# Requesting each weight piece of a fused attention and gated-MLP kernel as two transfers of unequal partition ranges

## The chip, the cores and the metric

The kernel runs on one core of one Trainium2 chip. The metric is the device time of one execution in microseconds (us). Three runs of the kernel before gave 142.08, 142.20 and 143.18 us; their median is 142.2 us.

## The reference, cut to what matters

```python
def _attn_ref(q, k, v, alpha):            # 4 batches, 8 heads, 768 steps, 48 wide
    state = zeros((B, H, D, D)); y = zeros_like(q)
    for t in range(S):
        state = alpha[:, :, t, :, None] * state + einsum('bhd,bhe->bhde', k[:, :, t], v[:, :, t])
        y[:, :, t] = einsum('bhd,bhde->bhe', q[:, :, t], state)
    return y

def _moe_ref(x, w_in, w_spatial, b_spatial, w_out):   # x is y as (4, 768, 384)
    h = maximum(x @ w_in, 0.0)                        # w_in (384, 1024)
    u, v = h[..., :512], h[..., 512:]
    v_n = (v - mean(v)) / sqrt(var(v) + 1e-06)        # over the last axis
    v_s = einsum('ts,bsd->btd', w_spatial, v_n) + b_spatial[None, :, None]   # w_spatial (768, 768)
    return (u * v_s) @ w_out                          # w_out (512, 384)
```

All inputs and the output are float32.

## The kernel before, in words

The first half is a gated linear attention. It is computed in 24 chunks of 128 steps, six to each of the four batches. For each chunk the kernel reads alpha (tile `ac`), k (`kc`), q (`qc`) and v (`vc`). The first eight chunks are read two at a time, with 384 KB in a request (L432); the others are read singly, with 192 KB (L637). ScalarE takes the logarithm of alpha (`la`), TensorE sums it over time, ScalarE makes exponentials of the sums (`binvp` or `binv`), GpSimd or VectorE scales k with them (`kt`), VectorE scales q (`qt`), TensorE transposes both, multiplies them (`ptm` is the masked product), and carries a running state from chunk to chunk (`state`, `sbd`).

The second half is a gated MLP on the four batches: x times `w_in` (columns 512 to 1023 give v, columns 0 to 511 give u), a normalisation of v, a product with `w_spatial` over time, a bias, a product with u, and a product with `w_out`. It is interleaved with the attention of later chunks.

The weights are read once, in six pieces of 768 KB each: the half of `w_in` for v, then the half for u, then `w_spatial` in three pieces of 256 rows, then `w_out` (L1067 to L1073). The function `fetch` (L1076) handles one piece. Its inner function `load` (L1081) takes a tile named `raw_w` of 128 partitions and 6 KB a partition, and requests the whole piece with one DMA on the SP queue (L1084). The source is a view of 128 partitions by n rows: n is 3 with runs of 512 numbers (2 KB) for `w_in`, 2 with runs of 768 numbers (3 KB) for `w_spatial`, and 4 with runs of 384 numbers (1.5 KB) for `w_out`. Then n copies (`cast`, L1090) turn the piece into bf16, one for each of the n rows, on ScalarE, VectorE or GpSimd. Each cast covers all 128 partitions. The pool `raws` has two buffers for `raw_w` (L160, NRAW = 2), so the third piece can be requested only when the casts of the first are done, and so on. After the last piece the same buffers serve as output tiles. The `w_spatial` casts give rows named `w_row`, which TensorE transposes at L831 into `w_spT`; the spatial product of the first batch needs them all.

The order of the instructions on every engine is written out by hand. The string PLAN (L57) is a list of words such as `S109 Q110`: a letter for the engine and the number of an operation. `replay` (L112) issues the operations in that order. An operation that requests a DMA is an S word, and the SP queue issues its requests in the order of the S words. The six weight pieces stand at places 10, 15, 18, 19, 24 and 31 of the 111 requests of the SP queue. All other requests of that queue are reads of ac, kc, qc and vc and stores of the output. The requests use eight completion semaphores in turn: each request waits, on the SP queue, until the request eight places before it has landed. An instruction that reads a tile waits for the semaphore of the request that filled it.

Of the kernel before, what the change touches and what calls it, by code (L numbers as in the profile page):

```python
# [124 lines left out]
def kernel(  # L125
# [12 lines left out]
    nc = tc.nc  # L138
# [57 lines left out]
    def copy(eng, out, in_):  # L196
        if eng == "ACT":
            nc.scalar.copy(out=out, in_=in_)  # L198
        else:
            ENG[eng].tensor_copy(out=out, in_=in_)  # L200
# [84 lines left out]
    def op(key, *args, **kw):  # L285

        users = kw.pop("use", ())
        o = Op(key, *args, **kw)
        for s in users:
            s.users.append(o)  # L290
        ops.append(o)
        made[key] = o
        return o

    def got(*keys):
        return [made.get(x) for x in keys]

    def dma(key, us, emit, deps, prio, eng="SP", issue=0.99, lat=1.9):
        o = op(key + ("issue",), eng, issue, emit, deps, prio=prio)
        return op(key, "DMA", us, lambda _: None, [o], prio=prio, lat=lat)  # L300
# [775 lines left out]
    def fetch(key, prio, to, src):  # L1076

        n, cols = src.shape[1], src.shape[2]
        hold = {}

        def load(_):  # L1081
            flat = raws.tile([128, n * cols], FP32, name="raw_w")
            hold["w"] = flat.rearrange("p (n f) -> p n f", n=n)
            nc.sync.dma_start(out=hold["w"], in_=src)  # L1084

        dma(key, WT, load, list(fetched[-NRAW] if len(fetched) >= NRAW else []), prio, issue=0.68)
        for j in range(n):
            tt = 2 * key[-1] + j if to is None else None

            def cast(eng, j=j, tt=tt):  # L1090
                if to is None:
                    wsp_nat[tt] = raws.tile([128, S], BF16, name="w_row", bufs=NROW)
                copy(eng, wsp_nat[tt] if to is None else to[:, j, :], hold["w"][:, j, :])

            op(("cast",) + key + (j,), {"POOL": 0.02 + 0.0012 * cols, "ACT": 0.11 + 0.00073 * cols, "DVE": 0.07 + 0.00104 * cols},
               None, cast, got(key), prio=prio + 12)
            if to is None:
                casts.append((made[("cast",) + key + (j,)], tt))
        made[key] = [made[("cast",) + key + (j,)] for j in range(n)]
        fetched.append(made[key])  # L1100
# [59 lines left out]
```

## Time and profile before

| What | Value |
|---|---|
| median of three runs | 142.2 us (142.08 to 143.18) |
| the profiled execution, its own time | 142.43 us |
| span of the profiled execution, first to last instruction | 140.6 us |
| time around the span | 1.8 us |
| granted TensorE clock, mean | 0.997 of full speed |
| TensorE (PE) busy | 135.3 us, 96% of the span |
| VectorE (DVE) busy | 118.5 us, 84% |
| ScalarE (ACT) busy | 108.1 us, 77% |
| GpSimd (POOL) busy | 83.9 us, 60% |
| moved by DMA | 28.64 MB, mean 204 GB/s |

All times in the profile are microseconds from the start of the span unless marked ns. The busy figure of TensorE includes matmuls on a tile named `junk`, whose results nobody reads. PE is TensorE's matmul, PEld its weight load, and SPq is the queue that issues the requests. A row of the timeline gives start, duration, engine, source line, operation, tiles (written, then read), shape, count, and in brackets the idle time of the engine before it and what ended that idle time. For a request on SPq the duration is the time that it held the queue; the time from its start to its landing stands in the view of DMA issues. The row of 40 digits gives, for 40 equal slices of the span of 3.5 us each, how busy something was in tenths.

### The profile page before, as it was taken

Reading aid. Unit: us, or ns where it says so; the run is one execution under the profiler, and the core shown is the slowest. Engines: PE = TensorE matmul, PEld = TensorE weight load, DVE = VectorE, ACT = ScalarE, POOL = GpSimd, SP = SyncE. Lnnn points to the kernel's source line nnn. Section 1 sums busy time; section 2 is a strip of 40 time slices with the busy share of each in tenths; the row PEclk is TensorE's granted clock in tenths of the full one; section 3 lists DMA queues with packets and bytes.
Section 4 is the critical chain, followed back from the end, with each engine's and each line's share of the span. In section 5 each row is a group of like instructions: output and inputs, shape, how many; then the busy total and the mean of one; then the engine's idle time right before and its main releaser. Section 6 shows DMA issues by size and latency. Waiting matters only on the chain.

```text
span 140.6 us, 4974 instructions
## 1 busy us (share of the span) xinstructions
PE 135.3 (96%) x1921; PEld 84.1 (60%) x1921; DVE 118.5 (84%) x292; ACT 108.1 (77%) x279; POOL 83.9 (60%) x148
## 2 busy tenths in 40 slices
PE   7999999999999999999999999999999999999990
PEld 3357566574767656665665765656657666566560
DVE  7187799989999789899689999999899899987850
ACT  3487898899976678999989699989967978751021
POOL 6816458861469996970289999402788599002520
PEclk9999999999999999999999999999999999999998
DMA  4999997989999979989999998999999120005535
GB/s 101 320 324 328 338 254 245 295 286 315 267 226 161 306 145 215 203 175 210 188 199 190 188 200 171 199 200 220 257 222 225 71 107 7 0 23 212 215 146 192
DMA packets 89000, 28.64 MB, mean 204 GB/s; under 512 B 83728, under 2 KB 87440, under 8 KB 88976
## 3 DMA queue, kind: packets, MB, share of 16 engines
q1 hardware_dynamic: 88944, 28.32, 81.8%
q8 instruction: 15, 0.25, 0.7%
q14 instruction: 9, 0.07, 0.2%
q0 software_dynamic: 32, 0.00, 0.0%
HBM read 23.60 MB, written 4.72 MB: 201 GB/s over the span
## 4 chain that ended last, share of the span: by engine, by line
PE 59%; ACT 9%; DMA 9%; SPq 7%; POOL 5%; DVE 5%; issue 4%; ACTq 0%; POOLq 0%
PE bank L819 42%; SPq L432 7%; DMA raw_w<-in_moe_w_in_dram 5%; DMA ac<-in_alpha_dram 3%; PE bank L710 3%; PE bank L745 2%; PE bank L773 2%; PE bank L731 2%; PE bank L657 2%; PE bank L767 1%; POOL kt L681 1%; DMA out_dram<-raw_w 1%; PE bank L389 1%; POOL kt L474 1%; ACT vn L880 1%
## 5 line engine op out<-in xcount | busy, mean ns | idle before, releaser
L819 PE MATMUL bank<-w_spT,vn 128*128 128x384 bf16 x192 | 35.9, 326 | 0.0
L980 POOL TENSOR_TENSOR gT<-vsb,uT 128x384 bf16<-128x384 f32 x27 | 25.0, 939 | 12.5 <-DVE vsb L967 12.1
L819 PEld LDWEIGHTS <-vn 128*128 128x128 bf16 x192 | 17.3, 97 | 10.2
L681 POOL TENSOR_TENSOR kt<-kc,binv 128x384 bf16<-128x384 f32 x16 | 14.6, 917 | 11.9 <-ACT bc L676 7.3
L756 DVE TENSOR_TENSOR ptm<-bank,mask 128x512 bf16<-128x512 f32 x32 | 20.5, 680 | 0.7 <-PE bank L745 0.6
L819 PE MATMUL bank<-xT,w_in 128*128 128x384 bf16 x96 | 19.9, 326 | 0.0
L967 DVE TENSOR_TENSOR vsb<-bank,bsp_bc 128x384 f32<-128x384 f32 x31 | 16.6, 551 | 3.6 <-PE bank L819 3.0
L819 PE MATMUL bank<-w_in,xT 128*128 128x512 bf16 x72 | 18.8, 379 | 0.3 <-ACT xT L198 0.2
L819 PE MATMUL bank<-w_out_sb,gT 128*128 128x384 bf16 (+1 forms) x100 | 18.6, 320 | 0.0
L198 ACT COPY kqT<-bank 128x512 bf16<-128x512 bf16 x28 | 15.9, 598 | 2.2 <-PE bank L710 1.5
L335 POOL TENSOR_TENSOR state<-state,bc 128x192 f32<-128x192 f32 x20 | 10.1, 506 | 12.4 <-DVE mvs L896 5.5
L200 POOL CAST sbd<-state 64x192 bf16<-64x192 f32 x40 | 13.7, 341 | 2.1
L204 ACT ACTIVATE v_sb<-bank 128x512 bf16<-128x512 f32 x20 | 12.0, 602 | 2.4 <-PE bank L819 2.3
L884 DVE BATCH_NORM_STATS2 stats<-v_sb 128x6 f32<-128x512 bf16 x20 | 13.6, 682 | 0.0
L204 ACT ACTIVATE uT<-bank 128x384 bf16<-128x384 f32 x23 | 10.9, 492 | 2.2 <-PE bank L819 2.0
L819 PEld LDWEIGHTS <-w_in 128*128 128x128 bf16 x96 | 8.7, 97 | 5.9
L198 ACT COPY xT<-bank 128x192 bf16<-128x192 bf16 (+1 forms) x25 | 9.0, 377 | 4.1 <-PE bank L389 2.9
L819 PEld LDWEIGHTS <-gT 128*128 128x128 bf16 x100 | 8.8, 97 | 5.0
L188 PE MATMUL bank<-junk 128*128 128x512 f32 (+6 forms) x22 | 10.7, 613 | 1.1 <-DVE junk L1050 1.1
L585 DVE TENSOR_TENSOR ptm<-bank,mask 128x512 bf16<-128x512 f32 x16 | 10.3, 682 | 1.0 <-PE bank L574 1.0
L198 ACT CAST x_sb<-bank 128x384 bf16<-128x384 f32 x19 | 9.0, 494 | 2.3 <-PE bank L773 2.3
L916 DVE TENSOR_SCALAR vn<-v_sb,mvs,rstd 128x512 bf16<-128x512 bf16 x24 | 8.9, 404 | 1.5 <-ACT rstd L909 1.5
(129 smaller groups left out, 281.2 us busy)
## 6 DMA issues: line engine op xcount, KB each, us to landing
ac<-in_alpha_dram SPq DMA_DIRECT2D x16, 192.0 KB, 4.0
kc<-in_k_dram SPq DMA_DIRECT2D x16, 192.0 KB, 4.0
qc<-in_q_dram SPq DMA_DIRECT2D x16, 192.0 KB, 4.2
vc<-in_v_dram SPq DMA_DIRECT2D x16, 192.0 KB, 4.0
raw_w<-in_moe_w_spatial_dram SPq DMA_DIRECT2D x3, 768.0 KB, 5.5
out_dram<-raw_w SPq DMA_DIRECT2D x11, 192.0 KB, 2.9
out_dram<-o_sb SPq DMA_DIRECT2D x9, 192.0 KB, 1.9
ac<-in_alpha_dram SPq DMA_DIRECT2D x4, 384.0 KB, 4.6
```

What stands on the lines that cost most here:

```text
L188: nc.tensor.matmul(out=flat[:, 0:cols].rearrange("p (a b) -> p a b", a=4), lhsT=junk, rhs=junk[:, None, 0:n].to_broadcast([128, 4, n]), st ...
L198: nc.scalar.copy(out=out, in_=in_)
L200: ENG[eng].tensor_copy(out=out, in_=in_)
L204: nc.scalar.activation(out=out, in_=in_, func=AF.Relu)
L335: ENG[eng].tensor_tensor(out=st["state"], in0=st["state"], in1=st["bc"][:, :, None].to_broadcast([128, HP, D]), op=ALU.mult)
L585: nc.vector.tensor_tensor(out=st[f"ptm{par}"][:, s], in0=st[f"pt{s}{par}"], in1=mask2[:, par], op=ALU.mult)
L681: ENG[eng].tensor_mul(out=k_blocks(kt3)[:, :, :, 0:D], in0=quad(st["kc"]), in1=st["binv"])
L756: nc.vector.tensor_tensor(out=st["ptm"][:, s], in0=st[f"pt{s}"], in1=mask4, op=ALU.mult)
L819: return lambda ps: nc.tensor.matmul(out=out(ps), lhsT=lhsT(), rhs=rhs(), start=start, stop=stop)
L884: nc.vector.bn_stats(out=stats, in_=d["v_sb"][:, tt, :])
L967: nc.vector.tensor_tensor(out=hold["vs"], in0=ps[:, 0:TH], in1=bsp_bc[:, th, :], op=ALU.add)
L980: ENG[eng].tensor_tensor(out=bt[b]["gT"][:, dsl, cols], in0=hold["vs"], in1=bt[b]["uT"][:, dsl, cols], op=ALU.mult)
```

## The change

In `load`, the one request of a piece becomes two, of partitions 0 to 79 and of partitions 80 to 127. Both write the same `raw_w` tile. Everything else stays: the string PLAN, the buffers, the casts and their engines.

```diff
         def load(_):
             flat = raws.tile([128, n * cols], FP32, name="raw_w")
             hold["w"] = flat.rearrange("p (n f) -> p n f", n=n)
-            nc.sync.dma_start(out=hold["w"], in_=src)
+            for rows in (slice(0, 80), slice(80, 128)):
+                nc.sync.dma_start(out=hold["w"][rows], in_=src[rows])

         dma(key, WT, load, list(fetched[-NRAW] if len(fetched) >= NRAW else []), prio, issue=0.68)
```

A piece of 768 KB is then requested as 480 KB and 288 KB, back to back. The SP queue has 117 requests in place of 111. No other engine's instructions change in number, shape or order; each cast waits for two completion semaphores in place of one, and because six requests more take part in the turn of eight semaphores, every later request waits for a request that lies fewer places back in the old count where weight requests lie in between.

## The prediction

> **What bounds the kernel now.** I read the page first, for the slices of the span and the chain that ended last.
>
> ```profile
> DMA  4999997989999979989999998999999120005535
> PE bank L819 42%; SPq L432 7%; DMA raw_w<-in_moe_w_in_dram 5%; DMA ac<-in_alpha_dram 3%; PE bank L710 3%; PE bank L745 2%; PE bank L773 2%; PE bank L731 2%; PE bank L657 2%; PE bank L767 1%; POOL kt L681 1%; DMA out_dram<-raw_w 1%; PE bank L389 1%; POOL kt L474 1%; ACT vn L880 1%
> ```
>
> The reader is to see that the DMA engines are full up to slice 31 (109 us) and that one weight transfer, the first half of w_in, stands on the chain. The chain in order of time says where.
>
> ```profile
> 10.29 6.88 DMA raw_w<-in_moe_w_in_dram
> 17.19 0.62 ACT w_in L198
> ...
> 34.12 0.95 DVE w_row L200 x2
> 35.12 0.52 PE bank L831 x24
> 35.64 1.08 PE bank L819 x6
> ```
>
> So the start is paced by transfers, up to the first weight cast at 17.19. From there a run of ScalarE, GpSimd and VectorE work leads to the transposes of w_spatial at 35.12, and then TensorE is the chain almost without a break to 62 us. What delays the casts before 43 us delays TensorE. Next the timeline, for the casts that wait for a piece, and the SP queue's rows.
>
> ```profile
> 17.19 0.62 ACT L198 CAST w_in<-raw_w 128x512 bf16<-128x512 f32 x1 [0.34 <-DMA raw_w<-in_moe_w_in_dram]
> ...
> 26.22 0.61 POOL L200 CAST w_in<-raw_w 128x512 bf16<-128x512 f32 x1 [0.25 <-DMA raw_w<-in_moe_w_in_dram]
> ```
>
> ```profile
> 10.29 1.33 SPq L1084 DMA_DIRECT2D raw_w<-in_moe_w_in_dram  x1
> 11.66 0.49 SPq L432 DMA_DIRECT2D kc<-in_k_dram  x1
> 12.20 1.06 SPq L432 DMA_DIRECT2D qc<-in_q_dram  x1
> 13.31 3.73 SPq L432 DMA_DIRECT2D vc<-in_v_dram  x1
> ```
>
> The two idle times, 0.34 and 0.25 us, are all that an earlier landing of w_in could give back. The queue issues far ahead of the data: the qc requested at 12.20 lands 8.0 us later.
>
> **Where a piece lands.** The view of DMA issues, window by window, gives the time from issue to landing. I add it to the issue's start. The alpha before the first piece lands at 9.02 + 5.0 = 14.0, the piece at 10.29 + 6.9 = 17.2: 3.2 us for 768 KB. The second (alpha 17.16 + 5.4 = 22.6, piece 18.28 + 7.8 = 26.1) takes 3.5. The first w_spatial piece (kc 20.64 + 7.8 = 28.4, piece 23.25 + 7.2 = 30.4) takes 2.0. The second (28.78 + 4.3 = 33.1) comes 2.7 later, about 0.65 of it because its request waited for a cast. So a piece needs 2.0 us of the DMA engines at best, and the w_in pieces 1.2 and 1.5 more.
>
> **The change part by part.**
>
> *Six more issues on SP.* The shortest rows of a weight issue and of its neighbour are 0.37 and 0.43 us, so 6 x 0.4 = 2.4 us of the SP queue. I cost them at nothing: behind the first piece the requests land 6.6 to 8.0 us after issue, behind the second w_spatial piece 5.1, so the DMA engines have several transfers in hand while SP issues. If that cover were gone it would be 0.4 each, 2.4 in all.
>
> *The turn of eight semaphores.* With the extra requests, a request waits for one that lies six or seven places back in the old count. The closest case I find is the qc at 35.54, which would wait for the second w_spatial piece's second half; the whole piece landed at 33.1, so 2.4 us are spare. Cost nothing; should the landing come over 2.4 us later than SP, it is that excess.
>
> *A second wait on each cast.* The parts land in order, so the first has landed when the second does. Nothing, apart from the instruction that carries the wait.
>
> *The transfers themselves.* No row of this trace shows a transfer of 80 or of 48 partitions. From below: five stores of 192 KB, issued back to back from 128.48 to 130.46, land between 128.48 + 4.0 = 132.5 and 130.46 + 3.9 = 134.4, so 768 KB in four requests take 1.9 us. By that row a further request is free: 0. A gain is limited by the idle times above to 0.34 + 0.25 = 0.6 us in all. From above: each part takes as long as a whole good piece, so 2.0 us more. Between them I take 0.8 us more for each piece: nearer to the lower end because the first w_spatial piece shows no loss beside the best rate, and not at it because the w_in reads, in the same queue, show that a request can lose 1.2 to 1.5 us over that rate; two requests of unequal size have two such occasions.
>
> *How 0.8 us reaches the end.* I keep two sums: how late the queue is, and how late the engines are.
> 1. First w_in piece: the cast starts when it lands. Queue 0.8, engines 0.8.
> 2. Second w_in piece: queue 1.6. GpSimd's cast starts 0.1 after landing, and GpSimd has 0.2 idle before its next kt (28.96). Engines 1.6 - 0.3 = 1.3.
> 3. First and second w_spatial pieces: queue 1.6 + 0.8 - 0.65 (the gap above) + 0.8 = 2.55. The cast of the second starts at 34.51, 1.4 after landing; 2.55 - 1.4 = 1.15 is under 1.3. Engines 1.3.
> 4. Third w_spatial piece: queue 3.35. It landed at 34.62 + 5.5 = 40.1; ScalarE's cast started 0.6 later and ended 1.0 before its transposes at 42.54, so about 1.5 spare. Engines 3.35 - 1.5 = 1.85.
> 5. w_out: queue 3.35 + 0.8, less about 1 us of idle DMA in slice 11 (the digit 7). Its first cast (51.1) comes 2.2 after its landing (48.9). Nothing new. The later reads wait in their tiles for 1.7 us or more in nearly all cases, so the queue's remaining lead of 1.3 over the engines is covered.
>
> Sum: 142.43 + 1.85 = 144.3 us against the profiled execution, which lies 0.2 above the median of the runs shown.
>
> [...]
>
> **The rivals.**
>
> *The request is free* (not slower). The pieces land where they did. For it: the stores' row, and the long queue that hides SP's issues. Against: nothing in the trace, only that no such ranges occur. 142.4; up to 0.5 us a piece it stays within 1%, since then the second w_in piece gives 0.7 and the w_spatial pieces hide: 143.1.
>
> *Each part takes as long as a whole piece*, as it would if 80 or 48 partitions used only part of the paths into the tile. Price 2.0 a piece. Queue 2.0, 4.0, then 7.35 and 9.35; engines 2.0, 3.7, 5.95 and 9.35 - 1.5 = 7.85. That is 150.3. For it: the best piece, 768 KB in 2.0 us or 393 GB/s, is the fastest read of the run, so there is little to spare. Against: parts back to back can overlap, and the w_in pieces are not at that rate to begin with. [...]
>
> *The w_in pieces lose their excess* (faster). Smaller requests, other rows to each DMA engine, and the 1.2 and 1.5 us vanish. It gives at most the 0.6 us of idle time: 141.8. Other causes, ScalarE busy up to 16.85 among them, come next.
>
> **How the numbers follow.** About 1% is what a measurement of this kernel can tell from no change. Chances: my forecast, with 0.5 to 1.4 us a piece (143.1 to 147.3 by the same sums), 0.50; the free request 0.32; the full doubling 0.12; the faster one 0.06. The range leaves out the doubling and most of the faster case: 142.0 to 147.5. Faster by over 1% means under 140.8, beyond what the idle times can give: 0.04. Within 1% is the free request, most of the faster case and the lowest part of mine: 0.38. Slower is the rest: 0.58. The likeliest case's own range is 143.1 to 147.3.
>
> **What would show it.** In the changed kernel's profile: the first w_in piece's second part landing near 18.0 rather than 17.2, ScalarE's idle time before its cast growing from 0.34 to about 1.1, the w_row casts about 1.3 later, TensorE's run from 35 on shifted by as much and L831's last transposes by nearly 2. If the cast stays at 17.2, the free request is right; if it starts at 19 or later, the doubling. The forecast fails if the parts' loss overlaps with work in the queue that I count as full.

## The result, and the profile after

The changed kernel takes 149.14 us (median of six runs, 147.95 to 150.86) where the kernel before takes 142.16 us in its runs on the same chip. The ratio is 1.0448, with a 95% interval of 1.039 to 1.0505. Two of the six runs (150.19 and 150.86 us) are slow ones, which the ratio leaves out; the other four have a median of 148.6 us. That is slower, as forecast, but 4.3 us over the predicted 144.3 and 1.1 us above the top of the range (4.8 and 1.6 by the median of all six).

The first profiled execution took 150.19 us. In it TensorE stood still for 2.4 us near 27 us and then ran at half clock (last section). A second profiled execution of the same kernel, called the second look below, shows neither and takes 149.25 us, so that stop is not the cause. I read the profile after off the second look. These are the row of DMA activity and the chain by line on its page.

```profile
DMA  4999999999999899999999999897989941005635
PE bank L819 33%; DMA raw_w<-in_moe_w_spatial_dram 6%; SPq L637 6%; DMA raw_w<-in_moe_w_in_dram 5%; DMA ac<-in_alpha_dram 5%; DMA kc<-in_k_dram 3%; PE bank L188 3%; SPq L1085 2%; PE bank L710 2%; PE bank L745 2%; POOL kt L681 2%; PE bank L773 2%; PE bank L767 2%; SPq L432 2%; PE bank L657 1%
```

A slice is now 3.7 us wide in place of 3.5, and the DMA engines are full for 32 slices in place of 31. The full stretch ends near 118 us instead of 109, for the same 28.64 MB. On the chain, TensorE's L819 has fallen from 42% to 33%. Waits for w_spatial pieces are new on it with 6%, and waits for alpha have risen from 3% to 5% (9% in the first execution).

This is the timeline of the second look, at the casts that wait for a piece, and the transposes of the last w_spatial rows. The brackets hold the idle time of the engine and what ended it.

```profile
17.86 0.62 ACT L198 CAST w_in<-raw_w 128x512 bf16<-128x512 f32 x1 [0.92 <-DMA raw_w<-in_moe_w_in_dram]
...
28.65 0.61 POOL L200 CAST w_in<-raw_w 128x512 bf16<-128x512 f32 x1 [1.90 <-DMA raw_w<-in_moe_w_in_dram]
...
37.15 0.56 DVE L200 CAST w_row<-raw_w 128x768 bf16<-128x768 f32 x1 [0.91 <-DMA raw_w<-in_moe_w_spatial_dram]
...
39.85 0.56 DVE L200 CAST w_row<-raw_w 128x768 bf16<-128x768 f32 x1 [1.35 <-DMA raw_w<-in_moe_w_spatial_dram]
...
47.62 0.83 ACT L198 CAST w_row<-raw_w 128x768 bf16<-128x768 f32 x1 [1.46 <-DMA raw_w<-in_moe_w_spatial_dram]
...
49.10 0.34 PE L831 MATMUL bank<-ident,w_row 64*128 64x64 bf16 x12
```

The first two stand in the prediction with 17.19 and 26.22. These are the others in the kernel before; the row of two casts holds the one that begins at 34.51.

```profile
33.25 0.55 DVE L200 CAST w_row<-raw_w 128x768 bf16<-128x768 f32 x1
34.05 1.01 DVE L200 CAST w_row<-raw_w 128x768 bf16<-128x768 f32 x2
...
40.70 0.84 ACT L198 CAST w_row<-raw_w 128x768 bf16<-128x768 f32 x1
...
43.15 0.34 PE L831 MATMUL bank<-ident,w_row 64*128 64x64 bf16 x12
```

They are late by 0.7, 2.4, 3.9, 5.3, 6.9 and 5.95 us. From cast to cast the lateness grows, and each of the five casts in the second look waits for its transfer; of these w_spatial casts none did before. The span grows by 6.9 us (140.6 to 147.5).

The busy times by stretch show the same from TensorE's side: first the kernel before, then the second look. The columns are the stretch, its length, the busy time of PE, PEld, DVE, ACT and POOL, the granted clock, the busy share of the DMA engines, and what they moved.

```profile
20.00:30.00 10.00, 9.49 (x220) 6.64 (x218) 9.14 (x21) 9.12 (x24) 8.84 (x21) 1.00 0.94 281
30.00:40.00 10.00, 9.77 (x179) 6.35 (x177) 9.86 (x27) 9.38 (x28) 3.03 (x5) 1.00 1.04 281
40.00:50.00 10.00, 9.96 (x177) 6.56 (x176) 8.89 (x22) 6.75 (x16) 9.21 (x16) 1.00 0.97 216
```

```profile
20.00:30.00 10.00, 9.04 (x208) 6.17 (x211) 7.55 (x18) 8.04 (x21) 7.28 (x17) 1.00 1.05 237
30.00:40.00 10.00, 5.84 (x60) 3.58 (x58) 6.14 (x16) 7.65 (x19) 3.00 (x6) 1.00 1.02 200
40.00:50.00 10.00, 9.11 (x226) 6.27 (x227) 9.51 (x24) 6.50 (x17) 5.99 (x11) 1.00 0.99 199
```

From 30 to 40 us TensorE loses 3.9 us of busy time, at full clock. The DMA engines count as busy in both kernels (1.04 and 1.02), but move 200 GB/s in place of 281. So for nearly all of this stretch they don't wait for requests to be issued: they are occupied, and the same bytes occupy them longer. The exception is its last microsecond, in which the busy share is 0.27:

```profile
39.00:40.00 1.00, 0.00 (x0) 0.00 (x0) 0.15 (x1) 0.66 (x2) 0.09 (x1) 1.00 0.27 51
```

### The profile page after: what moved, and what is told of

Same layout as the page of the kernel before. It is cut to its first block, busy times and chain, and to the rows that moved or that the text cites. A ratio compares the mean times of both kernels' runs of the same rounds, so it can differ in the third digit from the quotient of the medians.

```text
span 148.4 us, 4974 instructions
## 1 busy us (share of the span) xinstructions
PE 135.9 (92%) x1906; PEld 84.9 (57%) x1921; DVE 119.0 (80%) x292; ACT 108.7 (73%) x279; POOL 84.0 (57%) x148
## 2 busy tenths in 40 slices
DMA packets 89096, 28.64 MB, mean 193 GB/s; under 512 B 83824, under 2 KB 87536, under 8 KB 89072
## 4 chain that ended last, share of the span: by engine, by line
PE 50%; DMA 15%; ACT 9%; SPq 8%; POOL 8%; issue 6%; DVE 3%; ACTq 0%; POOLq 0%; DVEq 0%
PE bank L819 34%; DMA ac<-in_alpha_dram 9%; SPq L432 6%; DMA raw_w<-in_moe_w_in_dram 5%; POOL kt L681 2%; PE bank L745 2%; POOL sbd L200 2%; PE bank L710 2%; ACT la L651 2%; ACT uT L204 2%; PE bank L773 1%; SPq L1085 1%; PE bank L657 1%; PE bank L767 1%; PE bank L574 1%
## 5 line engine op out<-in xcount | busy, mean ns | idle before, releaser
L819 PE MATMUL bank<-w_spT,vn 128*128 128x384 bf16 x192 | 35.9, 326 | 0.0
L819 PEld LDWEIGHTS <-vn 128*128 128x128 bf16 x192 | 17.3, 97 | 10.2
L819 PE MATMUL bank<-xT,w_in 128*128 128x384 bf16 x96 | 19.9, 326 | 0.0
L819 PE MATMUL bank<-w_in,xT 128*128 128x512 bf16 x57 | 17.5, 401 | 1.5 <-ACT xT L198 0.7
L819 PE MATMUL bank<-w_out_sb,gT 128*128 128x384 bf16 (+1 forms) x100 | 18.6, 320 | 0.0
L819 PEld LDWEIGHTS <-w_in 128*128 128x128 bf16 x96 | 8.7, 97 | 5.9
L819 PEld LDWEIGHTS <-gT 128*128 128x128 bf16 x100 | 8.8, 97 | 5.0
L188 PE MATMUL bank<-junk 128*128 128x512 f32 (+6 forms) x22 | 10.2, 588 | 1.1 <-DVE junk L1050 1.1
```

Of the source, the lines that this page charges most:

```text
L188: nc.tensor.matmul(out=flat[:, 0:cols].rearrange("p (a b) -> p a b", a=4), lhsT=junk, rhs=junk[:, None, 0:n].to_broadcast([128, 4, n]), st ...
L819: return lambda ps: nc.tensor.matmul(out=out(ps), lhsT=lhsT(), rhs=rhs(), start=start, stop=stop)
```

## Experiments

Four theories were to be told apart. *A*: a request for part of the partitions moves its bytes at a lower rate. *B*: every further request costs, whatever its shape. *Q*: the DMA engines are the bound up to 109 us, so queue time that is lost counts wherever it is lost. *L*: what counts is only when a piece itself lands against its cast, as the prediction's steps have it. A loss in us below is the ratio less 1, times the median of the runs of the kernel before that were taken beside it (142.5 to 142.9 us).

### The number of requests, and where the cut lies

The first kernel requests each piece in two parts by rows of the piece. Each part covers all 128 partitions, and each cast waits for its own part alone.

```diff
-            for rows in (slice(0, 80), slice(80, 128)):
-                nc.sync.dma_start(out=hold["w"][rows], in_=src[rows])
+            cut = (n + 1) // 2
+            for js in (slice(0, cut), slice(cut, n)):
+                nc.sync.dma_start(out=hold["w"][:, js], in_=src[:, js])
```

> Two requests for each piece as in the changed kernel, but split by the n rows (2 and 1, 1 and 1, 2 and 2) and each of all 128 partitions. Theory A, the ranges of partitions: a transfer of 80 or 48 partitions moves its bytes at a lower rate. Then this one costs nothing: 141.6 to 142.8 us, and the first w_in piece's last part lands near 17.2. Theory B, the number of requests (issues on SP, the turn of eight semaphores, completions): then this one is as slow as the changed kernel, 147 to 150 us. Each cast here waits for its own part alone, which can give back up to the 0.6 us of idle time before the w_in casts.

Measured: 143.23 us, ratio 1.0038 (1.0001 to 1.0076), a loss of 0.5 us against 6.4. It has the same 117 requests on SP and the same turn of semaphores as the changed kernel. The time lies above the 142.8 that A allowed, but the kernel before took 142.93 beside it. Its first cast begins at 18.16 in its profile, and not near 17.2 as expected; that profile is of the slowest of its ten runs (145.13 us). B falls: by the interval at most 1.1 us of the 6.4 can belong to the number of requests, and at most 0.6 more if the casts' earlier start hides some. The rates below put a further request at 0.12 us.

The second cuts the partitions in the middle.

```diff
-            for rows in (slice(0, 80), slice(80, 128)):
+            for rows in (slice(0, 64), slice(64, 128)):
```

> The changed kernel with the cut at 64 in place of 80. Theory A, if what counts is how many of the paths into a tile a range reaches, and a half reaches half of them: each part takes as long as a whole piece, as slow as the changed kernel or slower, 148 to 152 us. [...] Theory B: the same as the changed kernel, 147 to 150.

Measured: 149.55 us, ratio 1.0407 (1.031 to 1.0504), a loss of 5.8 us. It cannot be told from the cut at 80. Unequal sizes are not needed for the loss.

### Which pieces

Two kernels split the change: `w_in` alone, and everything else alone.

```diff
+            for rows in (slice(0, 80), slice(80, 128)) if key[0] == "w_in" else (slice(0, 128),):
```

> Only the two w_in pieces are split at 80. By the sums of the prediction, with the measured size, they bring the first 1.9 us at the first cast (17.2 to 19.1 in the changed kernel) and nearly nothing more at the second: 144 to 145 us if the rest of the loss belongs to the w_spatial and w_out pieces; 147 or more if the loss between 27 and 35 us (a TensorE stall and a lower clock) comes with the late w_in pieces.

Measured: 144.84 us, ratio 1.0138 (1.0076 to 1.02), a loss of 2.0 us (1.1 to 2.9) for two pieces.

```diff
+            for rows in (slice(0, 80), slice(80, 128)) if key[0] != "w_in" else (slice(0, 128),):
```

> Only the three w_spatial pieces and w_out are split at 80. By the sums of the prediction the w_spatial pieces' loss shows where the spare time of 1.4 and 1.5 us ends: 143.5 to 146 us. If the TensorE stall at 27 us comes from the late w_in pieces it is absent here, and the granted clock stays at 0.99 or above.

Measured: 146.97 us, ratio 1.028 (1.0228 to 1.0332), a loss of 4.0 us (3.3 to 4.7) for four pieces, 1 us above the 146 that were expected at most. The two losses add up to 6.0, near the 6.4 of the whole. These four pieces, which the prediction hid for the most part, carry more of the loss than the two of `w_in`.

Then `w_out` alone, which the prediction costs at nothing.

```diff
+            for rows in (slice(0, 80), slice(80, 128)) if key[0] == "w_out" else (slice(0, 128),):
```

> Only w_out is split at 80. Its casts start 2.2 us after it lands in the kernel before, so by step 5 of the prediction the split costs nothing: 142.0 to 142.8 us. Theory Q: the DMA engines are the bound up to 109 us, and time lost in their queue is lost at the end wherever it is lost: 1 to 1.5 us more, 143.2 to 144.2.

Measured: 143.49 us, ratio 1.0048 (1.0009 to 1.0087), a loss of 0.7 us (0.1 to 1.2). Beside a kernel before of 142.2 us the ratio makes that 142.9, between the two forecasts: small, but not nothing. In its profile the first `w_out` cast begins at 51.05, no later than before (51.15). So as far as this profile goes, what loss there is does not come by way of the piece's own casts. The three w_spatial pieces are then left with 3.3 of the 4.0 (2.4 to 4.2).

The first `w_in` piece alone, of which steps 1 and 2 speak:

```diff
+            for rows in (slice(0, 80), slice(80, 128)) if key == ("w_in", 1) else (slice(0, 128),):
```

> Only the first w_in piece is split at 80. The rates measured alone give 1.4 us for it, and step 1 of the prediction says that it counts in full, since the cast starts when the piece lands: 143.5 to 144.2 us. If only the sum of the queue counts, with one piece of six, about 1.1 us more.

Measured: 143.72 us, ratio 1.0078 (1.0049 to 1.0108), a loss of 1.1 us (0.7 to 1.5). The interval holds the 1.4 of step 1 and the 1.1 of the sum alike, so this run does not tell them apart.

### The second look

The changed kernel, profiled once more.

> The changed kernel once more, for a second profile. If TensorE's stop of 2.4 us at 27 us and the low clock after it belong to the change, both are there again; if they are of that one execution, the span is nearer to 146 us with the clock at 1.0.

Measured: 149.25 us, mean granted clock 1.0. The stop and the low clock are not there, so the change does not always bring them; but the span is 147.5 us and not near 146. Its lines are those shown above.

### The price of a request, by itself

This kernel leaves the whole computation out. It only reads w_spatial pieces into four buffers, stage by stage. A stage is four pieces of one form, and a small copy on VectorE waits for the last of them before the next stage may write. The stages in order: whole; 80 + 48; 64 + 64; two rows of 128 partitions; 0 to 79 alone; 80 to 127 alone; 0 to 31 alone; 0 to 63 alone; 64 to 127 alone; 96 + 32; 112 + 16; whole.

```python
for a, z in stage:
    nc.sync.dma_start(out=buf[a:z, i], in_=piece[a:z])
```

> Not the computation: it only reads pieces of w_spatial into one tile, in twelve stages of four pieces each with a wait between stages, and stores 192 KB. Stages: whole pieces; 80 and 48 partitions; 64 and 64; two rows of all 128; 80 alone; 48 alone (80 to 127); 32 alone; 0 to 63 alone; 64 to 127 alone; 96 and 32; 112 and 16; whole again. Theory A in the form that a range's rate goes by the paths that it reaches: whole 2.0 us a piece, 64 and 64 about 3.8, 80 and 48 about 3.0 to 3.6, two rows 2.0; 32 partitions alone at the same rate in bytes as 64 alone, about half of the whole's. Theory A in the form that unequal work for the DMA engines costs: 64 and 64 at 2.0 and 80 and 48 more. Theory B, a cost for each request: two rows as slow as 80 and 48.

Measured, first the rate in 40 slices of 3.8 us from the page, then the timeline of the small copies. The idle time in brackets is the length of a stage: issue, latency and four pieces.

```profile
GB/s 0 0 251 414 176 233 231 237 127 141 232 224 223 50 345 404 107 271 195 123 147 43 208 70 221 127 135 209 73 224 244 247 120 208 248 261 121 291 410 186
```

```profile
33.85 0.17 DVE L45 COPY tiny<-buf 128x8 f32<-128x8 f32 x1 [16.14 <-DMA buf<-in_moe_w_spatial_dram]
50.64 0.17 DVE L45 COPY tiny<-buf 128x8 f32<-128x8 f32 x1 [16.62 <-DMA buf<-in_moe_w_spatial_dram]
61.78 0.17 DVE L45 COPY tiny<-buf 128x8 f32<-128x8 f32 x1 [10.97 <-DMA buf<-in_moe_w_spatial_dram]
71.88 0.17 DVE L45 COPY tiny<-buf 128x8 f32<-128x8 f32 x1 [9.93 <-DMA buf<-in_moe_w_spatial_dram]
81.79 0.17 DVE L45 COPY tiny<-buf 128x8 f32<-128x8 f32 x1 [9.74 <-DMA buf<-in_moe_w_spatial_dram]
87.70 0.17 DVE L45 COPY tiny<-buf 128x8 f32<-128x8 f32 x1 [5.74 <-DMA buf<-in_moe_w_spatial_dram]
...
124.03 0.17 DVE L45 COPY tiny<-buf 128x8 f32<-128x8 f32 x1 [15.55 <-DMA buf<-in_moe_w_spatial_dram]
138.70 0.17 DVE L45 COPY tiny<-buf 128x8 f32<-128x8 f32 x1 [14.49 <-DMA buf<-in_moe_w_spatial_dram]
149.35 0.17 DVE L45 COPY tiny<-buf 128x8 f32<-128x8 f32 x1 [10.48 <-DMA buf<-in_moe_w_spatial_dram]
```

Whole pieces move at 410 to 414 GB/s, so a piece of 786,432 bytes takes 1.9 us; pieces in 80 + 48 move at 231 to 237 GB/s, 3.4 us. The stage lengths give the price without the latency. For 80 + 48 it is (16.14 - 10.48) / 4 = **1.42 us a piece**, for 64 + 64 1.54 (3.4 us in all, where the first form of A had about 3.8), for 96 + 32 1.27, for 112 + 16 1.00, and for two rows of 128 partitions 0.12. A holds. The most telling stages are the parts alone: 80 partitions need 9.93 and 48 partitions 9.74, nearly as long as a whole piece (10.48), while 32 partitions (0 to 31) need 5.74. Either half alone needs 10.02 (0 to 63) and 10.24 (64 to 127). The time does not go by the bytes. Two parts in a row cost 1.42 more and not 1.9 more, so they overlap a little. Only w_spatial pieces were read here; that the `w_in` and `w_out` pieces, whose rows are shorter, have the same price is assumed in the tables below.

### Where the partitions lie

Why should 48 partitions take as long as 80? One answer is that their number sets the rate (A2 below); another is that their place counts. This kernel, which leaves the computation out as well, reads ranges of equal size at different places: whole; 32 to 95; 0 to 63; 32 to 79; 80 to 127; 48 to 79; 0 to 31; 16 to 111; three requests of 32 to 95, 0 to 31 and 96 to 127; whole.

> Not the computation: stages of four reads of w_spatial pieces again, with other ranges of partitions. [...] Theory A2, the number of partitions, or of rows dealt to each DMA engine, sets the rate: 32 to 95 as 0 to 63 and 32 to 79 as 80 to 127, 1.9 to 2.0.

Measured, the timeline of its small copies, as above:

```profile
25.20 0.17 DVE L43 COPY tiny<-buf 128x8 f32<-128x8 f32 x1 [7.55 <-DMA buf<-in_moe_w_spatial_dram]
35.22 0.17 DVE L43 COPY tiny<-buf 128x8 f32<-128x8 f32 x1 [9.86 <-DMA buf<-in_moe_w_spatial_dram]
41.94 0.17 DVE L43 COPY tiny<-buf 128x8 f32<-128x8 f32 x1 [6.54 <-DMA buf<-in_moe_w_spatial_dram]
51.88 0.17 DVE L43 COPY tiny<-buf 128x8 f32<-128x8 f32 x1 [9.77 <-DMA buf<-in_moe_w_spatial_dram]
57.80 0.17 DVE L43 COPY tiny<-buf 128x8 f32<-128x8 f32 x1 [5.75 <-DMA buf<-in_moe_w_spatial_dram]
63.55 0.17 DVE L43 COPY tiny<-buf 128x8 f32<-128x8 f32 x1 [5.58 <-DMA buf<-in_moe_w_spatial_dram]
74.70 0.17 DVE L43 COPY tiny<-buf 128x8 f32<-128x8 f32 x1 [10.98 <-DMA buf<-in_moe_w_spatial_dram]
89.18 0.17 DVE L43 COPY tiny<-buf 128x8 f32<-128x8 f32 x1 [14.31 <-DMA buf<-in_moe_w_spatial_dram]
99.47 0.17 DVE L43 COPY tiny<-buf 128x8 f32<-128x8 f32 x1 [10.12 <-DMA buf<-in_moe_w_spatial_dram]
```

48 partitions from 32 to 79 need 6.54, and 48 partitions from 80 to 127 need 9.77: 0.81 us a request between them, with the same bytes and the same shape. 64 partitions from 32 to 95 need 7.55, and from 0 to 63 9.86. So it is the place that counts, and A2 falls. The three requests need 14.31 against 10.12 for the whole, 1.05 us a piece: less than 80 + 48 with its two requests, so once more it isn't the number. The place is not all, though: for 0 to 31, 48 to 79, 32 to 79 and 32 to 95 the stages grow with the size: 5.58, 5.75, 6.54 and 7.55. By the difference to the whole, 32 to 95 takes 1.26 us a request (1.9 - (10.12 - 7.55) / 4). The 96 partitions from 16 to 111 need 10.98, a little more than the whole. The rows of the source lie elsewhere too; that was not separated from the place in the tile. By what mechanism the place counts was not shown.

### Queue time or landing

Two kernels leave the pieces whole and add a read of 384 KB of q to each, into a spare tile that nobody reads: behind the piece in one, ahead of it in the other. The output tiles of the pool `outp` become one tile that the spare reads share.

```diff
-            for rows in (slice(0, 80), slice(80, 128)):
-                nc.sync.dma_start(out=hold["w"][rows], in_=src[rows])
+            nc.sync.dma_start(out=hold["w"], in_=src)
+            spare.append(spare.pop(0))
+            nc.sync.dma_start(out=spare[0], in_=spare_src)
```

> The kernel before, with whole pieces, and behind the request of each piece a second request that reads 384 KB of q into the output tiles that are still free; nobody uses those bytes. 117 requests, as in the changed kernel. Such a read takes 1.2 us of the DMA engines, the split 1.4. Theory Q, time lost in the queue counts wherever it is lost: 147 to 149 us. Theory L, what counts is that each piece itself lands late: here no piece has its own loss, only those of the pieces ahead of it, so 144 to 146.

Measured: 149.28 us, ratio 1.0453 (1.0411 to 1.0495), a loss of 6.5 us.

> The same idle read, but ahead of each piece, so that the piece itself lands 1.2 us later. Theory Q: as the one behind. Theory L: as slow as the changed kernel, 147.5 to 149.5, and at least 1.5 us slower than the one behind.

Measured: 149.26 us, ratio 1.0429 (1.0357 to 1.0501), a loss of 6.1 us. Behind costs as much as ahead, which speaks for Q and against L. The test is weaker than meant. In the profiles the first cast begins at 18.58 with the read behind and at 17.63 with the read ahead (17.19 before), the other way round from what the edit was to do to the first piece. The shared output tile was not tried without the reads. Still, both kernels reproduce the whole slowdown with no request for part of the partitions.

The last kernel changes the dose.

```diff
-            for rows in (slice(0, 80), slice(80, 128)):
+            for rows in (slice(0, 112), slice(112, 128)):
```

> The changed kernel cut at 112. Alone, a piece took 2.9 us in this cut, 3.4 in the cut at 80 and 1.95 whole. If the loss goes by that price, two thirds of the changed kernel's: 146 to 147.5 us. By the steps of the prediction with 0.95 a piece: 145. If any cut costs the same, 148.5.

Measured: 146.93 us, ratio 1.0266 (1.0202 to 1.033), a loss of 3.8 us.

Prices and losses side by side, with the interval of each loss. The price of the q reads is an estimate: in the kernel before, requests of that size follow each other by 1.2 us at the start.

| Kernel | DMA time added, us | loss of device time, us | loss per us added |
|---|---|---|---|
| first `w_in` piece | 1.42 | 1.1 (0.7 to 1.5) | 0.8 |
| both `w_in` pieces | 2.84 | 2.0 (1.1 to 2.9) | 0.7 |
| w_spatial and `w_out` | 5.68 | 4.0 (3.3 to 4.7) | 0.7 |
| `w_out` | 1.42 | 0.7 (0.1 to 1.2) | 0.5 |
| 112 + 16, all | 6.0 | 3.8 (2.9 to 4.7) | 0.6 |
| 64 + 64, all | 9.2 | 5.8 (4.4 to 7.2) | 0.6 |
| 80 + 48, all (the change) | 8.5 | 6.4 (5.5 to 7.2) | 0.75 |
| q behind, all | 7.2 | 6.5 (5.9 to 7.1) | 0.9 |
| q ahead, all | 7.2 | 6.1 (5.1 to 7.1) | 0.85 |

By the middle values, half to nine tenths of the time lost reaches the end. All rows but those of the q reads fit a common 0.7, and the price of the q reads is the least certain. What takes up the rest was not settled. No version here beats the kernel before; the one by rows comes nearest with all six pieces in two requests, and it wins nothing.

## Why the prediction was wrong

**What held.** Six more issues on SP, the turn of eight semaphores and the second wait cost little: the version by rows has the first two and loses 0.5 us (0.0 to 1.1). Step 1 held in its form: that piece alone costs 1.1 us. The sign was right.

The sign that the prediction named, the start of the first cast, is worth less than it looks. In the second look it begins at 17.86 after 0.92 us of idle time, close to the 18.0 and 1.1 of the forecast. In the first profiled execution it began at 19.06 after 1.86, which the prediction had called the sign of the doubling. Over the profiles, it begins at 16.50, 16.62 and 17.19 where the first piece is whole, and at 17.68, 17.73, 17.86 and 19.06 where it is cut at 80. That is 1.2 us later by the medians, and one profile alone could have spoken for either case.

**The term that was too small: the transfers themselves.** I took 0.8 us a piece between bounds of 0 and 2.0; it is 1.42 for a w_spatial piece read by itself, just above the 1.4 where I let my own case end. I leaned to the lower end because of the stores, 768 KB in four requests in 1.9 us. That row shows that a *request* is cheap, and the version by rows confirms it. But each of those stores covers all 128 partitions, so it said nothing of a request for part of them, and there was no nearer row. That goes the way of the rival to which I gave 0.12: a part read alone takes nearly as long as a whole piece (stages of 9.93 and 9.74 us against 10.48). The paths into the tile, its explanation, were a guess that no run shows. Its 150.3 came near for a reason that was half wrong: a price that was too high (2.0 where 1.42 was measured, as the parts overlap), with the cover of steps 3 to 5 that was too generous. That the two errors nearly cancel is luck.

**What hides a lost microsecond.** With 1.42 the prediction's own steps can be tried on the experiments:

| Pieces cut | by the steps, us | measured, us |
|---|---|---|
| first `w_in` | 1.42 | 1.1 (0.7 to 1.5) |
| both `w_in` (steps 1, 2) | 2.84 - 0.3 = 2.5 | 2.0 (1.1 to 2.9) |
| w_spatial (steps 3, 4) | 3 x 1.42 - 0.65 - 1.5 = 2.1 | 3.3 (2.4 to 4.2) |
| `w_out` (step 5) | 0 | 0.7 (0.1 to 1.2) |
| all | 5 x 1.42 - 0.65 - 1.5 = 4.95 | 6.4 (5.5 to 7.2) |

So of the 4.55 us that the forecast of 1.85 lacks, 3.1 (4.95 - 1.85) are the price. The other 1.45 (0.6 to 2.2) fall to the steps 3 to 5, since the steps 1 and 2 give rather too much. Those steps subtracted spare time: 0.65 us of a gap in the queue, 1.4 and 1.5 us between landing and cast, and everything at `w_out`. Such spare time covers a piece, not the queue behind it. The reads of ac, kc, qc and vc stand in the same queue and become late too, and some are wanted at once. The request right behind `w_out` shows it, an alpha: first its row in the kernel before, then the piece of the second look's chain.

```profile
43.74 0.51 SPq L637 DMA_DIRECT2D ac<-in_alpha_dram  x1
```

```profile
51.35 7.31 DMA ac<-in_alpha_dram
```

It is requested 7.6 us later and lands 7.3 us after its request in place of 5.9. Before, the only alpha on the chain is a later one, at 67.62, with 4.1 us. That the late reads are the carrier is read from this chain, and from the profile of `w_out` alone, whose first cast did not start later; no run took the reads out. "The queue's remaining lead is covered" is the sentence that failed, and it failed with the price: by the same steps the lead with 1.42 a piece is (6 x 1.42 - 0.65 - 1) - 4.95 = 1.9 us, more than the 1.7 us that the reads were said to wait in their tiles. How the 1.2 us that steps 3 and 4 lack are shared among their three subtractions was not measured.

One reading was wrong besides: the idle DMA that step 5 subtracts (the digit 7) is in slice 14, from 49 to 53 us, and not in slice 11. As the step gave nothing anyway, the sum is the same.

## What to carry to other kernels

Ask of a transfer which partitions it covers before asking how many requests it is: cut it along the free dimension and each request keeps all 128 partitions and nearly the full rate (0.12 us a piece here, against 1.42). Two halves of the partitions, 64 + 64, take 1.54 us a piece longer than the whole. Where the DMA engines are full for three quarters of the span, cost an edit by the DMA time that it adds, and let spare time at one consumer cover only that consumer.

## What was not expected of the hardware

In the first profiled execution of the changed kernel TensorE stood still and then ran at half clock. The columns are those of the stretches above.

```profile
27.00:28.00 1.00, 0.00 (x0) 0.00 (x0) 0.30 (x1) 0.00 (x0) 0.89 (x3) 1.00 1.14 275
28.00:29.00 1.00, 0.00 (x0) 0.00 (x0) 0.00 (x0) 0.00 (x0) 0.39 (x1) 0.64 1.01 274
29.00:30.00 1.00, 0.62 (x9) 0.56 (x10) 0.13 (x1) 0.00 (x0) 0.00 (x0) 0.50 0.79 170
...
34.00:35.00 1.00, 1.00 (x3) 0.15 (x1) 0.36 (x2) 0.84 (x2) 0.58 (x1) 0.50 0.65 184
35.00:36.00 1.00, 1.00 (x39) 0.86 (x39) 0.66 (x2) 0.67 (x2) 0.00 (x0) 0.95 1.11 286
```

TensorE stops in the middle of 16 matmuls of one form (11 before the stop, 5 behind it), and the profile names nothing that it waits for. The other engines then wait for it and run dry by 29 us, and the granted clock is at 0.5 from 29 to 35 us. The time of that execution, 150.19 us, is within 1 us of the second look's, which had a mean clock of 1.0, and 2.2 us above the fastest of the six. What six microseconds at half clock cost cannot be told from that spread. What stopped TensorE stays open.

A busy share near 1.0 says little of the rate that the DMA engines reach: from 30 to 40 us they moved 281 GB/s in the kernel before and 200 in the changed one, at busy shares of 1.04 and 1.02.
